# Which array shape TensorE's products take, and where attention's normalisation is written

## The chip, the core and the metric

One core of a Trainium2 chip. The metric is the device time of one execution in microseconds, the median over several runs; for a single run its one time. The engines are TensorE (PE, with PEld for its weight loads), VectorE (DVE), ScalarE (ACT), GpSimd (POOL) and the queue of SyncE (SP), which issues most DMAs. Each engine executes its instructions in the order of the program.

## The reference, cut to what matters

Attention inside clusters, and on its output a gated long convolution:

```python
# q, k, v: (4, 8, 768, 64); centroids: (8, 16, 64)
q_assign = argmax(q_n @ c_n.T); k_assign = argmax(k_n @ c_n.T)      # q_n, k_n, c_n: of unit length
mask = q_assign[:, :, :, None] == k_assign[:, :, None, :]
attn = softmax(where(mask, q @ k.T / 8, -1e9)); attn_out = attn @ v
x = attn_out.transpose(0, 2, 1, 3).reshape(4, 768, 512)
x1, x2, x3 = split(x @ w_proj, 3)
x2_conv = irfft(rfft(x2, axis=1) * rfft(filter_fft, axis=0), axis=1)
out = (x1 * x2_conv * x3) @ w_out
```

## The kernel before, in words

The 32 heads are taken in eight groups of four (n), each group in two pairs (pr), and in a pair the keys in six blocks of 128 (sk). The work is done in these steps.

Routing (`routing`, `first_masks`). Raw q and k are transposed on TensorE (`L570` in sixes, `L579` in threes), copied to SBUF (`qkT`) and cast to bf16 (`aug`). Products with the centroids (`sim`, L599) are copied out and transposed (`simT`, L610). VectorE makes one-hot rows of them (`oh`), TensorE transposes these (`ohT`), and DMAs set them into `aug` as extra rows, so that one product gives score and mask together.

Attention (`attention`). For each key block there are three score tiles of 512 columns (`sc`), three exponentials on ScalarE (`exp`, L695 and L698) into one of five buffers `p`, one group of value products in f32 (`pv`, L709, into a pair of PSUM banks, 4 and 5) and one addition into `acc` on VectorE (L719). After six blocks `acc` is summed over partitions (`den`, L732), and the pair is copied to `osb` (L724). The denominators are copied to SBUF. They go through DRAM to 12 columns, get eps added (L743), are inverted (L744), and come back through DRAM as rows over 64 partitions (`rb`). VectorE then adds eps to `osb` and multiplies it by `rb` in place (L780), and another instruction casts the result to bf16 as tokens (`xT`, line 789). The very last pair makes this turn on TensorE instead of through DRAM (L760, L765, L766, L772, L785).

Gated convolution (`hyena`), once for each batch b, behind its two head groups. `U` multiplies tokens by the middle third of w_proj (L817). `spectrum` is the forward transform (L464, L467). VectorE multiplies by the filter's spectrum (L841, L845). `G` gives the two gates, `I` the inverse transform, `fold` and L907 make `y2`, `W` is the output product. The first three batches' steps are spread among the attention of later groups. The last batch's steps come after all attention, so that the end of the program is a stage of its own, from the last `den` to the last output DMA.

The order of the work is drawn before anything is emitted. Every step is an `Op` with the engines it can run on and their costs, its inputs and outputs, its PSUM banks and a due time. `Plan.place` takes the steps one by one in simulated time: for the engine that can start first it takes the step with the earliest due time, with bonuses. On TensorE a step in another array shape than the last one is charged `switch`, and its due time is put off by `shape`. Six banks serve scores and all other products, at most four each; banks 4 and 5 are lent to early steps (class `head`) and are then the pair for `pv`.

TensorE's array is used in three shapes: whole (128 x 128) for transposes, in two halves (128 x 64) for `pv`, scores, projections and transforms, in four quarters (128 x 32) for `sim` and `den`. In halves, `columns` issues two matmuls for the two halves of the output rows, and they run beside each other:

```python
def columns(out, lhsT, rhs, start, stop):
    for i in range(2):
        tensor.matmul(out[64 * i:64 * i + 64], lhsT[:, 64 * i:64 * i + 64], rhs, start=start, stop=stop)
```

All helper calls of this kind are recorded under L63. A group of transposes takes up to three ready scores with it (`together`, `MIX`): their pieces of 256 columns are issued between the transposes with the whole array (L674, `woven`).

Of the kernel before, what the change touches and what calls it, by code (L numbers as in the profile page):

```python
# [35 lines left out]
MIX = 3  # L36
# [4 lines left out]
MODES = {"pv": (64, 64), "score": (64, 64), "bc": (64, 64), "inv": (64, 64), "proj": (64, 64), "sim": (32, 32),  # L41
         "den": (32, 32)}


class Op:
    __slots__ = ("eng", "fn", "due", "deps", "outs", "left", "ready", "end", "start", "on",
                 "alloc", "free", "lat", "lock", "byts", "seq", "kind", "parts", "group", "fused", "span")
# [10 lines left out]
def halves(tensor):  # L58


    def columns(out, lhsT, rhs, start, stop):
        for i in range(2):
            tensor.matmul(out[64 * i:64 * i + 64], lhsT[:, 64 * i:64 * i + 64], rhs, start=start, stop=stop)  # L63
    return columns


class Plan:
# [6 lines left out]
    def op(self, eng, fn, due, r=(), w=(), alloc=None, free=(), lock=False, byts=0, after=(), kind=None,  # L74
           parts=None):
# [4 lines left out]
        o.parts, o.group, o.fused = parts, [], False  # L80
# [22 lines left out]
    def place(self, free0, banks_for, switch=0.1, wait=0.1, rate=215e3, bonus=2.592, margin=0.43, shape=0.553):  # L103
# [26 lines left out]

        def together(o, t):

            for x in sorted((x for x in ready["PE"] if x.kind == "score" and x.ready <= t), key=lambda x: (x.due, x.seq)):
                ids = banks_for(x.alloc, bank_free, st, x)
                if ids is None or ids[1] > t or len(o.group) == MIX:
                    break
                take(x)
                x.fused = True
                o.group.append(x)
            a, b = len(o.parts), sum(len(x.parts) for x in o.group)  # L140
            return max(.056 * a + .109 * b, .108 * a + .055 * b) + (.05 if b else .14)
# [29 lines left out]
        while any(ready.values()):  # L171
            best = None
            for e, lst in ready.items():
# [14 lines left out]
                if not cand:  # L188
# [4 lines left out]
                    + (shape if e == "PE" and MODES.get(c[1].kind, (128, 128))[0] != st.last else 0.0)  # L193
# [8 lines left out]
            if e == "PE":  # L202
                mode, ends = MODES.get(o.kind, (128, 128))
                if o.parts and o.kind != "score":
                    d = together(o, t)
                o.span = d
                if mode != st.last:
                    d += switch
                st.last, st.kind = ends, o.kind
# [3 lines left out]
            for i, x in enumerate(o.group):  # L213
                done(x, e, t + 1e-6 * (i + 1), 0.0, t + d * (i + 1) / len(o.group))
# [3 lines left out]


def each(parts):  # L220
    def fn(e):
        for f in parts:
            f()
    return fn


def woven(a, b):

    out, i = [], 0
    for j, f in enumerate(b):  # L230
        out.append(f)
        while i * len(b) < (j + 1) * len(a):
            out.append(a[i])
            i += 1
    return out
# [27 lines left out]
def build(T):  # L263
# [3 lines left out]
    T0 = 10.36  # L267
    TAU1 = 3.298
    TAU2 = 3.626
# [11 lines left out]
    columns = lambda *a, **k: halves(T.nc.tensor)(*a, **k)  # L281
# [109 lines left out]
    def tables(got):  # L391
# [44 lines left out]
        for i in range(3):  # L436
            hs = [Bank("head"), Bank("head")]
            due = 34 + 4.0 * i
            for cs in range(2):
                op(("PE", .648), lambda e, i=i, cs=cs, h=hs[cs]: spectrum(ap(h), i, cs), due + 2 * cs, r=U2 + FW, w=[hs[cs]],  # L440
                   alloc=hs[cs], kind="proj")
# [111 lines left out]
    def routing(n):  # L553
# [5 lines left out]
        for u in range(8):  # L559
# [7 lines left out]
            if n > 1 and ch == 0:  # L567
                h = Bank(cls, 2)

                tr2 = [lambda i=i, s=s, h=h: T.nc.tensor.transpose(bank(h.ids[i // 3])[:, ts(i % 3, 128)], raw(s, i), T.ident)  # L570
                       for i in range(NT)]
                op(("PE", .80), each(tr2), due, r=[("qkraw", s, 0), ("qkraw", s, 1), "ident"], w=[h], alloc=h, parts=tr2)
# [3 lines left out]
            elif n < 2:  # L576
                h = Bank(cls)

                tr = [lambda t=t, s=s, ch=ch, h=h: T.nc.tensor.transpose(ap(h)[:, ts(t, 128)], raw(s, 3 * ch + t), T.ident)  # L579
                      for t in range(3)]  # L580
                op(("PE", .36), each(tr), due, r=[("qkraw", s, 0), ("qkraw", s, 1), "ident"], w=[h], alloc=h,
                   parts=tr if n else None)
                op(EV384 if n != 1 else {"ACT": .48}, lambda e, z=z, ch=ch, h=h: copy(e, T.qkT[z][:, ch], ap(h)[:, :384]),
                   due + .6, r=[h], w=[("qkT", z, ch)], free=[h])
# [8 lines left out]
        b0 = end - 23.512  # L593
# [9 lines left out]
        for ch in range(2):  # L603
# [6 lines left out]
        simT = [lambda i=i, h=h: T.nc.tensor.transpose(bank(h.ids[i // 3])[:, ts(i % 3, 128)],  # L610
                                                       T.sim[:, i // 3, ts(i % 3, 128)], T.ident) for i in range(NT)]
        op(("PE", .80), each(simT), b0 + 2.5, r=SIM + ["ident"], w=[h], alloc=h, parts=simT)
# [19 lines left out]
        def ohT(e, h=h):  # L632
            o = ap(h).bitcast(BF16)
            f = T.oh[:].rearrange("p a n c -> p (a n c)")
            for t in range(NT):
                for i in range(2):
                    c = 128 * t + 64 * i
                    T.nc.tensor.transpose(o[64 * i:64 * i + 64, ts(t, 128)], f[:, c:c + 64], T.identb)
# [16 lines left out]
    def attention(n, pr, sins):  # L655
# [7 lines left out]
        for sk in range(NT):  # L663
# [4 lines left out]
            for u in range(3):  # L668
                h = Bank("score")

                def piece(hp, c, lo, hi, sk=sk, h=h):
                    K = 80 if hp == 0 else 128
                    ag = T.augs[aset][pr][hp]
                    T.nc.tensor.matmul(ap(h)[:, c:c + hi - lo], ag[1][:K, ts(sk, 128)], ag[0][:K, lo:hi], start=True,  # L674
                                       stop=True)
                parts, c = [], 0
                for hp, lo, hi in THIRDS[u]:
                    parts += [lambda f=piece, a=(hp, c + x - lo, x, x + 256): f(*a) for x in range(lo, hi, 256)]
                    c += hi - lo

                def sc(e, u=u, sk=sk, h=h):
                    c = 0
                    for hp, lo, hi in THIRDS[u]:
# [5 lines left out]
                                                     for hp, _, _ in THIRDS[u]], w=[h], alloc=h, kind="score",  # L689
                   parts=parts)  # L690
# [44 lines left out]
        op(EV384, lambda e: copy(e, T.den, ap(h)[:, :384]), te + 1.5, r=[h], w=["den"], free=[h])  # L735
        if not last:
# [5 lines left out]
            def rec(e):  # L742
                T.nc.vector.tensor_scalar(T.dn, T.dn, EPS * S, None, op0=Alu.add)  # L743
                T.nc.vector.reciprocal(T.dn, T.dn)  # L744
            op(("DVE", .52), rec, te + 6, r=[], w=["dn"])
# [7 lines left out]
            rk, fr = [("rb", 0), ("rb", 1)], []  # L753
        else:
# [8 lines left out]
            def rec(e):  # L763
                V = T.nc.vector
                V.tensor_scalar(T.dn, ap(h2)[:, :384][:, ::32], EPS * S, None, op0=Alu.add)  # L765
                V.reciprocal(T.dn, T.dn)  # L766
            op(("DVE", .45), rec, te + 2.5, r=[h2], w=["dn"], free=[h2])
# [8 lines left out]
            fr = rk  # L776
        osv = lambda: T.osb[os][:, :, :384]
        eps = lambda: T.osb[os][:, 1, 384:385]
        if not last:
            op(("DVE", 1.05), lambda e: T.nc.vector.scalar_tensor_tensor(osv(), osv(), eps(), rbv(), op0=Alu.add,  # L780
                                                                         op1=Alu.mult),
               te + 12, r=rk, w=[("osb", os)], lock=True)
        else:
            for ch in range(2):
                op(("DVE", .6), lambda e, ch=ch: T.nc.vector.scalar_tensor_tensor(  # L785
                    osv()[:, ch], osv()[:, ch], eps(), ap(rk[ch])[:, :384], op0=Alu.add, op1=Alu.mult),
                   te + 4, r=[rk[ch]], w=[("osb", os)], free=[rk[ch]], lock=True)
        xs = b % 2
        op({"ACT": .83, "DVE": .55}, lambda e: copy(e, T.xT[xs][:, kt].rearrange("p (a b) -> p a b", a=2), osv()),
           te + 13 - 7 * last, r=[("osb", os)], w=[("xT", xs, kt)], lock=True)  # L790


    def hyena(b):
        xs = b % 2
        last = b == B - 1
        w0 = A(24 * (b + 1)) + 15.205
        w1 = A(24 * (b + 2)) + 7.046 if b < B - 2 else A(96) + 24.526
        if last:
            w0 = A(96) - 18.55
            w1 = w0 + 10  # L800
# [7 lines left out]
        for m in range(3):  # L808
            for w_ in range(2):
# [9 lines left out]
                if last and 2 * m + w_ < NU:  # L819
                    op(("PE", .647), lambda e, U=U: U(e, range(3)), due, r=XT[:3] + ["wpj"], w=[h], alloc=h, kind="proj")  # L820
                    op(("PE", .217), lambda e, U=U: U(e, range(3, 4)), due, r=[XT[3], h], w=[h], kind="proj")
                else:
                    op(("PE", .862), U, due, r=XT + ["wpj"], w=[h], alloc=h, kind="proj")
# [9 lines left out]
        for i in range(3):  # L833
            for cs in range(2):
# [4 lines left out]
                   w=[h], alloc=h, kind="proj")  # L839
# [223 lines left out]
def kernel(  # L1063
# [64 lines left out]
    for o in order:  # L1128
        if o.fused:
            continue  # L1130
        for x in [o] + o.group:
            if x.alloc is not None:
                psum.want(x.alloc)
        if o.group:
            each(woven(o.parts, sum((x.parts for x in o.group), [])))(o.on)
        else:
            o.fn(o.on)
# [30 lines left out]
```

The softmax here doesn't subtract the row's maximum and nothing guards it: scores larger than these inputs give would overflow.

## Time and profile before

| | |
|---|---|
| median of 8 runs | 402.72 us (401.63 to 404.54) |
| profiled execution | 402.58 us, its span 400.8 us |
| granted TensorE clock, mean over the span | 0.996 |
| busy TensorE / VectorE / ScalarE | 379.6 / 370.0 / 275.4 us |
| value products (L709) | 768 matmuls, 143.3 us busy |
| scores, projections, transforms (L63) | 69.1 + 51.9 + 23.7 us in the three largest groups |
| woven score pieces (L674) | 120 matmuls |
| casts of `osb` to `xT` | 15 on VectorE (560 ns each), 1 on ScalarE (832 ns) |
| eps added to 12 columns (L743, L765) | 16 on VectorE (165 and 161 ns) |

A line of a group names its line of code, engine, operation, tiles and shapes, the count, the busy time and the mean of one instruction, then the idle time before it and what ended it. A line of the timeline begins with start and length in microseconds. A shape such as 128*64 128x385 is that of the weights, then that of the moving data. The ends of matmuls are modelled, so their lengths overlap; the distances between starts are measured.

### The profile page before, as it was taken

How to read it: one execution, taken by the hardware profiler on the slowest of the kernel's cores; microseconds unless marked ns; L12 is line 12 of the kernel's file. 1: busy time of each engine (PE TensorE's matmuls, PEld its weight loads, DVE VectorE, ACT ScalarE, POOL GpSimd, SP SyncE). 2: the span in 40 equal slices, each digit the busy share in tenths (PEclk: the TensorE clock that was granted, in tenths of full speed). 3: DMA queues.
4: the chain of work that ended last, by engine and by line, in shares of the span. 5: the costliest groups of instructions: out<-in, count | busy, mean ns of one | idle time of the engine just before them, and what ended most of it. 6: DMA issues, size and time to landing. Idle time of an engine off the chain costs nothing.

```text
span 400.8 us, 8872 instructions
## 1 busy us (share of the span) xinstructions
PE 379.6 (95%) x3498; PEld 209.6 (52%) x3498; DVE 370.0 (92%) x513; ACT 275.4 (69%) x522; POOL 17.0 (4%) x55
## 2 busy tenths in 40 slices
PE   3989999999999999999999999999999999999963
PEld 2554553654455565654545565565555555645741
DVE  8899997988989999999899999998899999999992
ACT  4898778878855897677872778679855667523512
POOL 8700100000000000000000000000000000000000
PEclk9999999999999999999999999999999999999998
DMA  9939969118510433127522225104310101100304
GB/s 173 230 56 205 224 148 199 41 38 199 131 56 23 118 81 82 42 60 201 159 81 59 65 58 122 38 23 137 141 42 23 39 3 42 42 2 2 159 0 158
DMA packets 67233, 37.09 MB, mean 93 GB/s; under 512 B 56700, under 2 KB 62328, under 8 KB 67192
## 3 DMA queue, kind: packets, MB, share of 16 engines
q1 hardware_dynamic: 62856, 33.62, 32.2%
q0 software_dynamic: 1056, 2.10, 2.8%
q10 hardware_dynamic: 3280, 0.82, 1.1%
q8 instruction: 27, 0.44, 0.5%
q14 instruction: 14, 0.11, 0.1%
HBM read 30.66 MB, written 6.48 MB: 93 GB/s over the span
## 4 chain that ended last, share of the span: by engine, by line
PE 76%; DVE 13%; ACT 5%; issue 2%; DMA 1%; SPq 1%; POOL 0%; DVEq 0%; POOLq 0%; ACTq 0%
PE bank L63 28%; PE pair L709 27%; PE bank L817 5%; PE bank L674 3%; PE bank L570 3%; PE bank L599 3%; PE bank L732 2%; DVE acc L719 2%; ACT p L698 2%; PE bank L467 1%; PE bank L610 1%; DVE tm L841 1%; PE bank L493 1%; DMA rb<-dr 1%; DVE hm L454 1%
## 5 line engine op out<-in xcount | busy, mean ns | idle before, releaser
L709 PE MATMUL pair<-p,vraw 128*64 128x385 f32 x768 | 143.3, 489 | 0.0
L698 ACT ACTIVATE p<-bank 128x512 f32<-128x512 f32 x192 | 114.5, 619 | 29.6 <-PE bank L63 25.2
L719 DVE TENSOR_TENSOR acc<-p,acc 128x1536 f32<-128x1536 f32 x64 | 111.8, 1747 | 4.3 <-ACT p L698 2.9
L709 PEld LDWEIGHTS pair<-p,vraw 128*64 128x64 f32 x768 | 53.6, 136 | 44.9 <-issue 37.9
L63 PE MATMUL bank<-aug,aug 128*64 128x512 bf16 (+3 forms) x610 | 69.1, 327 | 1.4 <-DVE aug L536 0.7
L695 ACT ACTIVATE p<-bank 128x512 f32<-128x512 f32 x96 | 58.9, 613 | 4.2 <-PE bank L63 3.1
L63 PE MATMUL bank<-xT,wpj 128*64 128x384 bf16 x512 | 51.9, 327 | 0.1
L63 PEld LDWEIGHTS <-aug 128*64 128x64 bf16 (+1 forms) x610 | 35.3, 109 | 30.2 <-issue 17.5
L63 PEld LDWEIGHTS <-wpj 128*64 128x64 bf16 x512 | 28.0, 109 | 22.2 <-issue 13.4
L277 ACT COPY qkT<-bank 128x384 f32<-128x384 f32 x58 | 27.3, 498 | 10.5 <-PE bank L63 9.4
L63 PEld LDWEIGHTS <-y 128*64 128x64 bf16 x448 | 21.9, 110 | 17.2 <-issue 5.0
L719 DVE TENSOR_TENSOR acc<-p,p 128x1536 f32<-128x1536 f32 x16 | 28.0, 1752 | 1.8 <-ACT p L698 1.5
L674 PE MATMUL bank<-aug,aug 80*128 80x256 bf16 (+1 forms) x120 | 28.5, 274 | 0.1
L841 DVE TENSOR_TENSOR tm<-bank,hm 128x512 f32<-128x512 f32 x44 | 27.7, 681 | 0.0
L570 PE MATMUL bank<-ident,qkraw 128*128 128x128 f32 x144 | 27.1, 275 | 0.0
L63 PE MATMUL bank<-wout,y 128*64 128x512 bf16 x192 | 23.7, 381 | 3.3 <-DVE y L907 3.3
L277 ACT CAST aug<-qkT 64x768 bf16<-64x768 f32 x30 | 24.9, 831 | 2.6 <-DVE qkT L279 2.0
L817 PE MATMUL bank<-wpj,xT 128*64 128x512 bf16 x192 | 22.1, 380 | 1.0 <-DVE xT L279 1.0
L277 ACT COPY ob<-bank 128x512 f32<-128x512 f32 x20 | 11.5, 589 | 13.3 <-PE bank L63 13.2
L570 PEld LDWEIGHTS bank<-ident,qkraw 128*128 128x128 f32 x144 | 18.3, 141 | 3.8 <-issue 2.1
L279 DVE CAST aug<-qkT 64x768 bf16<-64x768 f32 x30 | 16.6, 552 | 2.4 <-ACT qkT L277 1.7
L724 ACT COPY osb<-pair 128x770 f32<-128x770 f32 x16 | 12.8, 800 | 8.6 <-PE pair L709 8.3
(145 smaller groups left out, 438.6 us busy)
## 6 DMA issues: line engine op xcount, KB each, us to landing
vraw<-in_v_dram SPq DMA_DIRECT2D x16, 384.0 KB
qkraw<-in_q_dram SPq DMA_DIRECT2D x30, 192.0 KB
qkraw<-in_k_dram SPq DMA_DIRECT2D x30, 192.0 KB
rb<-dr SPq DMA_DIRECT2D x30, 192.0 KB
out_dram<-ob SPq DMA_DIRECT2D x11, 512.0 KB
y<-in_moe_filter_fft_dram SPq DMA_DIRECT2D x4, 384.0 KB
wpj<-in_moe_w_proj_dram POOLq DMA_DIRECT2D x1, 1536.0 KB, 12.2
aug<-ohT SPq DMA_DIRECT2D x60, 24.0 KB
```

Of the source, the lines that this page charges most:

```text
L63: tensor.matmul(out[64 * i:64 * i + 64], lhsT[:, 64 * i:64 * i + 64], rhs, start=start, stop=stop)
L277: T.nc.scalar.copy(out, in_)
L279: (T.nc.vector if e == "DVE" else T.nc.gpsimd).tensor_copy(out, in_)
L570: tr2 = [lambda i=i, s=s, h=h: T.nc.tensor.transpose(bank(h.ids[i // 3])[:, ts(i % 3, 128)], raw(s, i), T.ident) for i in range(NT)]
L674: T.nc.tensor.matmul(ap(h)[:, c:c + hi - lo], ag[1][:K, ts(sk, 128)], ag[0][:K, lo:hi], start=True, stop=True)
L695: T.nc.scalar.activation(o, ap(h).rearrange("p (a b) -> p a b", a=2), Act.Exp, scale=0.125)
L698: T.nc.scalar.activation(flat(s)[:, lo:lo + 512], ap(h), Act.Exp, scale=0.125)
L709: T.nc.tensor.matmul(o[64 * hp:64 * hp + 64, ch, :385], T.vraw[vs][:, hp, sk * D:(sk + 1) * D], T.p[slots[sk]][:, hp, 384 * ch:384 * ch + ...
L719: T.nc.vector.tensor_tensor(T.acc[:], P_(t[0]), P_(t[1]) if len(t) == 2 else T.acc[:], op=Alu.add)
L724: op(("ACT", .83), lambda e: T.nc.scalar.copy(T.osb[os], two(ob)[:, :, :385]), te, r=[ob], w=[("osb", os)], free=[ob])
L817: T.nc.tensor.matmul(ap(h)[64 * i:64 * i + 64], T.xT[xs][:, kt, c:c + 64], T.wpj[:, kt, DM:2 * DM], start=kt == 0, stop=kt == ND - 1)
L841: op(("DVE", .68), lambda e, i=i, cs=cs, r=r, h=h: T.nc.vector.tensor_tensor(T.tm[r][:, cs], ap(h), hmrow(i, (0, 2, 2, 3)[2 * r + cs]), op ...
```

## The change

The weaving is taken out: `together`, `woven`, `each`, `MIX` and the 256-wide pieces go, and transposes are issued in plain groups. Scores, gates, output products, the first two spectra, the inverse transform and the transposes of the one-hot rows get no shape of their own: `array` gives them the shape that the step before left, where that is 128 or 64, and halves otherwise. `product` then issues one matmul on the whole array or two on halves. `U` and the third spectrum, whose two halves have different weights and moving data, stay in halves (kind `half`). The normalisation (L780, L785) writes `xT` in bf16 itself, and the cast goes. Eps is added where the denominators are copied out of PSUM, by an activation with a bias on ScalarE or an addition on VectorE, and L743 and L765 go. Some costs and due times of the planner are changed with it, so the order of the steps is drawn anew.

```diff
-MODES = {"pv": (64, 64), "score": (64, 64), "bc": (64, 64), "inv": (64, 64), "proj": (64, 64), "sim": (32, 32),
-         "den": (32, 32)}
+MODES = {"pv": 64, "bc": 64, "half": 64, "sim": 32, "den": 32, "score": 0, "proj": 0, "inv": 0}
+def array(o, last):
+    return MODES.get(o.kind, 128) or (last if last in (64, 128) else 64)
...
-def halves(tensor):
...
+def product(T, out, lhsT, rhs, start, stop):
+    if T.whole:
+        return T.nc.tensor.matmul(out, lhsT, rhs, start=start, stop=stop)
+    for i in range(2):
+        T.nc.tensor.matmul(out[64 * i:64 * i + 64], lhsT[:, 64 * i:64 * i + 64], rhs, start=start, stop=stop)
...
-    def place(self, free0, banks_for, switch=0.1, wait=0.1, rate=215e3, bonus=2.592, margin=0.43, shape=0.553):
+    def place(self, free0, banks_for, switch=0.1, wait=0.1, rate=215e3, bonus=2.592, margin=0.43, shape=0.33):
...
-                mode, ends = MODES.get(o.kind, (128, 128))
-                if o.parts and o.kind != "score":
-                    d = together(o, t)
-                o.span = d
+                mode = array(o, st.last)
                 if mode != st.last:
                     d += switch
-                st.last, st.kind = ends, o.kind
+                st.last, st.kind, o.whole = mode, o.kind, mode == 128
...
-    T0 = 10.36
-    TAU1 = 3.298
-    TAU2 = 3.626
+    T0 = 9.454
+    TAU1 = 3.31
+    TAU2 = 3.644
...
-                op(("PE", .80), each(tr2), due, r=[("qkraw", s, 0), ("qkraw", s, 1), "ident"], w=[h], alloc=h, parts=tr2)
+                op(("PE", .68), tr2, due, r=[("qkraw", s, 0), ("qkraw", s, 1), "ident"], w=[h], alloc=h)
...
-        b0 = end - 23.512
+        b0 = end - 24.593
...
-        op(EV384, lambda e: copy(e, T.den, ap(h)[:, :384]), te + 1.5, r=[h], w=["den"], free=[h])
+        def total(e):
+            if e == "ACT":
+                T.nc.scalar.activation(T.den, ap(h)[:, :384], Act.Copy, bias=EPS * S)
+            else:
+                T.nc.vector.tensor_scalar(T.den, ap(h)[:, :384], EPS * S, None, op0=Alu.add)
+        op(EV384, total, te + 1.5, r=[h], w=["den"], free=[h])
...
-            def rec(e):
-                T.nc.vector.tensor_scalar(T.dn, T.dn, EPS * S, None, op0=Alu.add)
-                T.nc.vector.reciprocal(T.dn, T.dn)
-            op(("DVE", .52), rec, te + 6, r=[], w=["dn"])
+            op(("DVE", .3), lambda e: T.nc.vector.reciprocal(T.dn, T.dn), te + 6, r=[], w=["dn"])
...
-        if not last:
-            op(("DVE", 1.05), lambda e: T.nc.vector.scalar_tensor_tensor(osv(), osv(), eps(), rbv(), op0=Alu.add,
-                                                                         op1=Alu.mult),
-               te + 12, r=rk, w=[("osb", os)], lock=True)
...
-        op({"ACT": .83, "DVE": .55}, lambda e: copy(e, T.xT[xs][:, kt].rearrange("p (a b) -> p a b", a=2), osv()),
-           te + 13 - 7 * last, r=[("osb", os)], w=[("xT", xs, kt)], lock=True)
+        xv = lambda: T.xT[xs][:, kt].rearrange("p (a b) -> p a b", a=2)
+        for a_ in [slice(0, 2)] if not last else [slice(0, 1), slice(1, 2)]:
+            op(("DVE", .6 if last else 1.05), lambda e, a_=a_: T.nc.vector.scalar_tensor_tensor(
+                xv()[:, a_], osv()[:, a_], eps(), ap(rk[a_.start])[:, :384].unsqueeze(1) if last else rbv(), op0=Alu.add,
+                op1=Alu.mult), te + (4 if last else 12), r=[("osb", os)] + (rk[a_] if last else rk), w=[("xT", xs, kt)],
+               free=rk[a_] if last else [], lock=True)
...
-        w0 = A(24 * (b + 1)) + 15.205
-        w1 = A(24 * (b + 2)) + 7.046 if b < B - 2 else A(96) + 24.526
+        w0 = A(24 * (b + 1)) + 18.221
+        w1 = A(24 * (b + 2)) + 14.861 if b < B - 2 else A(96) + 24.673
```

## The prediction

> **What bounds the kernel now.** I read the page first, its busy rows and its chain; then the groups by form; then the timeline at the places where the chain leaves TensorE.
>
> ```profile
> span 400.8 us, 8872 instructions
> PE 379.6 (95%) x3498; PEld 209.6 (52%) x3498; DVE 370.0 (92%) x513; ACT 275.4 (69%) x522; POOL 17.0 (4%) x55
> PEclk9999999999999999999999999999999999999998
> PE 76%; DVE 13%; ACT 5%; issue 2%; DMA 1%; SPq 1%; POOL 0%; DVEq 0%; POOLq 0%; ACTq 0%
> ```
>
> TensorE carries three quarters of the chain at the full granted clock; VectorE is nearly as busy but carries 13%. So one microsecond less on TensorE is one microsecond less where TensorE binds: from the first value product (31.2 us) to the last denominators (352.4). The head belongs to ScalarE, the end (347 to 389) half to VectorE. Two prices come from TensorE's timeline, read as start to next start, because ends are modelled:
>
> ```profile
> 151.28 1.46 PE L709 MATMUL pair<-p,vraw 128*64 128x385 f32 x8
> 152.58 0.82 PE L63 MATMUL bank<-xT,wpj 128*64 128x384 bf16 x8
> 155.20 1.46 PE L709 MATMUL pair<-p,vraw 128*64 128x385 f32 x8
> 156.58 1.50 PE L599 MATMUL bank<-qkT,cbd 128*32 128x384 f32 x16
> ...
> 150.30 0.27 PE L674 MATMUL bank<-aug,aug 128*128 128x256 bf16 x1
> 150.41 0.27 PE L570 MATMUL bank<-ident,qkraw 128*128 128x128 f32 x1
> 150.61 0.84 PE L63 MATMUL bank<-xT,wpj 128*64 128x384 bf16 x8
> ```
>
> The same eight value products take 1.30 us ahead of another 128x64 group and 1.38 ahead of a 128x32 one; after a woven transpose the next start is 0.11 us away in the same shape, 0.20 in another. Over all such pairs of the trace a change of shape costs 0.095 us. Woven pieces follow each other at 0.109 to 0.113 us, so weaving runs nothing beside anything: a 256-wide piece alone in two halves needs 0.107.
>
> Three waits matter besides: one bank release at 31, the routing at 64 to 67, the last tokens at 360.
>
> ```profile
> 30.48 0.65 ACT L277 COPY qkT<-bank 128x384 f32<-128x384 f32 x1
> 31.18 1.52 PE L709 MATMUL pair<-p,vraw 128*64 128x385 f32 x8
> 31.80 0.69 ACT L277 COPY qkT<-bank 128x384 f32<-128x384 f32 x1
> 64.45 1.48 PE L599 MATMUL bank<-qkT,cbd 128*32 128x384 f32 x10 [0.47 <-ACT qkT L277]
> 66.58 0.55 PE L610 MATMUL bank<-ident,sim 128*128 128x128 f32 x3 [0.17 <-DVE sim L279]
> 67.06 2.21 PE L63 MATMUL bank<-aug,aug 80*64 80x512 bf16 x18
> 354.35 0.56 DVE L279 CAST xT<-osb 128x768 bf16<-128x768 f32 x1
> 355.69 0.16 DVE L765 TENSOR_SCALAR dn<-bank 128x12 f32<-128x12 f32 x1
> 359.47 0.56 DVE L279 CAST xT<-osb 128x768 bf16<-128x768 f32 x1
> 360.08 2.13 PE L817 MATMUL bank<-wpj,xT 128*64 128x512 bf16 x18 [0.96 <-DVE xT L279]
> 361.41 0.68 DVE L830 TENSOR_TENSOR uv<-tm,bank 128x512 bf16<-128x512 f32 x1
> ```
>
> **The change part by part**, along the path first product (31.18) to last denominators (352.35) to end.
>
> *Array shapes.* In the issue order of the changed kernel TensorE changes shape 102 times instead of 123. Only the TensorE-bound stretch counts: 90 instead of 102. 12 x 0.095 = -1.1 us. In the head 8 instead of 17 changes lie beside ScalarE's exponentials: nothing, and at most -0.9 if that cover were gone.
>
> *No weaving.* In the stretch 58 of the 60 woven scores, 116 pieces, go from about 0.111 us to 0.107: -0.5 us.
>
> *Full-array products.* 89 product matmuls (44 scores and 8 projections or spectra) now use one 128x128 matmul where two 128x64 ones ran beside each other. No row shows a 512-wide one. Nearest are L674's full-array pieces: 0.109 us apart with weight loads of 0.097 in between, so the load is hidden even under a 256-wide piece. I take 0. The Trainium skill ("TensorE: Matmul & The Clock Gate", part 3, what overlaps and what doesn't) speaks against this: a weight load overlaps a running matmul only where the row group differs, and full-array matmuls share their row groups. By that rule some 65 of the 89 lie in the bound stretch and each shows its load: 65 x 0.097 = +6.3 us. The row is this kernel's own case, so it decides; the rule is a rival below. Below zero: two 512-wide half products also start 0.213 us after the pair before, the rate of one full product, so no gain is in sight.
>
> *Bank of the first value product.* The pair L709 writes needs banks 4 and 5, still lent to early transposes. Now the copy at 30.48 releases it, and L709 starts when it ends. In the new order the later transposed block, whose copy starts at 31.80, sits in bank 5, and ScalarE's order up to that copy is unchanged. The first product starts at about 31.80 + 0.65 = 32.4: +1.2 us. Queued behind it are the 96 value products and the score buffers they free. Ends: 0 (ScalarE gets there sooner) and +1.4.
>
> *Routing at 57 to 68.* By starts, TensorE stands 2.25 us here: 0.2 for the denominators, 1.2 around L599, 0.3 between the halves of L610, 0.5 for exponentials after ScalarE had waited 1.71 for scores. In the new order scores follow L599 directly and L610 comes 22 operations later, behind four value products. L610's waits go, and ScalarE starts earlier; the wait for L599's input stays: -0.9 us (ends -0.3 and -1.5).
>
> *Work moved across the borders.* One score (0.21) goes ahead of the first product, one L63 group of the last batch's gates (0.64) goes behind the last denominators: -0.85 for the stretch. Together: -1.1 - 0.5 + 1.2 - 0.9 - 0.85 = -2.15; last denominators at 350.2.
>
> *VectorE and the queues.* Off go 15 casts to xT (0.56), one on ScalarE (0.83), 16 eps additions (0.16): 11 us of VectorE. The normalisation now writes bf16: by rows L830 and L841, same size to bf16 and to f32, 681 ns each, that is free (ends 0 and 15 x 0.1, hidden all the same). Adding eps at the denominators' copy makes a ScalarE copy of 0.48 an activation; the exponentials, 0.61 against 0.585 for a copy of that size, say +0.03, at most +0.1, in front of DMAs. All that lies beside TensorE, except in the last stage. On SP the eight mask copies for the second head group pass one load of v whose first use is over 30 us later: nothing. POOL's queue is unchanged.
>
> *The last stage.* From last denominators to first U part with the last tokens took 7.7 us (352.35 to 360.08), VectorE's chain throughout. The two casts and the addition, 1.3 us, are gone, and one fold of 0.5 no longer sits between the two last normalisations. TensorE's own work becomes the limit: denominators 0.65, two gate groups 1.28, transposes 0.33, three U groups 1.92, broadcasts 1.28, four shape changes 0.38 = 5.8 us. So U comes 1.9 earlier. But the new order leaves two VectorE instructions of the batch before for after the U stage: L907 (0.87 by its pitch) and one L881 (0.47). They had filled VectorE's wait for U; now they stand in front of the chain that ends in the last y. -1.9 + 1.35 = -0.55. One od copy moves from ScalarE to VectorE (0 to +0.5; a wait of 0.43 for the twin copy on ScalarE follows, so 0). The tail gives -0.55 (ends -1.3 and +0.5).
>
> Sum: -2.15 - 0.55 = **-2.7 us**. The profiled execution took 402.58 us, span 400.8 and 1.8 around it, 0.14 below the median of 402.72. 402.58 - 2.7 = 399.9.
>
> **The rivals.**
>
> *Late again elsewhere* (2 in 10). Every engine issues in order, and the order was drawn anew everywhere. At 224 us TensorE lost 0.26 to one late VectorE instruction. Ten such places, or one exponential chain late by 2 us, would leave 400.9 to 402.8. For: VectorE 92% busy. Against: it gets 11 us of air, and TensorE hardly waits from 70 to 345.
>
> *Weight loads shown* (7 in 100). The rule above holds for full products: +6.3 - 2.7 = +3.6, 406.2. It decides from 28 exposed loads in the bound stretch on (28 x 0.097 = 2.7). Against: L674's spacing.
>
> *More than summed* (15 in 100). The bank comes free as early as now (-1.2), the routing wait goes whole (-1.35): 397.4. For: both steps were priced with care on the dear side. Against: the position of the copy in ScalarE's order is plain.
>
> *It does nothing to the shapes*: excluded by the counts of the issue order.
>
> **How the numbers follow.** The main case has 58 in 100: 398.3 to 401.5 by the ends of its steps. A difference of 0.3%, 1.2 us, is about what a measurement of this kernel tells from no change. Faster: 56 of the main case, 15 of the third rival, 5 of the first: 76. Same: 2 and 13: 15. Slower: 7 and 2: 9. The range leaves out about 1 in 10 on each side: 397.0 to 403.0.
>
> **What would show it.** In the changed profile: about 100 shape changes, full-array score matmuls spaced 0.213 us at 512 wide (0.31 would be the rule); the first L709 at 32 to 32.5; scores directly behind the routing product near 64; the last denominators near 350; no cast to xT, U within 6 us of the denominators; VectorE 359 us busy. Wrong it is if the first product is on time, if TensorE waits between 70 and 345 for more than 2 us, or if the stretch from U to the last y grows by more than 1.4.

## The result and the profile after

| | before | after |
|---|---|---|
| median | 402.85 us (401.11 to 404.83, 32 runs) | 399.92 us (398.41 to 402.16, 11 runs) |
| ratio, 95% interval | | 0.9936 [0.9921, 0.9952] |
| profiled execution, its span | 402.58, 400.8 us | 399.49, 397.7 us |
| first value product | 31.18 us | 31.60 us |
| last denominators | 352.35 us | 347.95 us |
| first `uv` of the last batch (U with the last tokens done) | 361.41 us | 355.01 us |
| last wait for `y` ends | 389.03 us | 384.26 us |
| last matmul | 393.59 us | 390.50 us |

The median is 2.9 us lower, and in the pair of profiles the difference is 3.1 us. The forecast was 399.9. The stages did not go as forecast, though: the last denominators came 2.25 us earlier than said, and behind them 1.85 us of that was lost again. From the page of the changed kernel, its busy row, clock row and the shares of the chain:

```profile
span 397.7 us, 8781 instructions
PE 378.1 (95%) x3447; PEld 205.0 (52%) x3447; DVE 360.8 (91%) x485; ACT 274.4 (69%) x518; POOL 17.1 (4%) x55
PEclk9999999999999999999999999999999999999988
PE 90%; DVE 5%; ACT 3%; issue 1%; POOL 0%; POOLq 0%; DVEq 0%; ACTq 0%
```

VectorE lost 9 us of work, TensorE 1.5; the chain runs 90% through TensorE where it ran 76%. New is the 8 in the last but one slice of the clock: the granted clock fell inside the work. The places that had waits before, in the timeline (start, length, then in brackets the idle time before it and what ended it):

```profile
31.09 0.45 ACT L244 COPY qkT<-bank 128x384 f32<-128x384 f32 x1
31.60 1.52 PE L668 MATMUL pair<-p,vraw 128*64 128x385 f32 x8 [0.95 <-ACT qkT L244]
...
63.00 1.79 PE L567 MATMUL bank<-qkT,cbd 128*32 128x384 f32 x16
64.72 2.48 PE L68 MATMUL bank<-aug,aug 80*64 80x512 bf16 x24
```

The first value product (L668, in the kernel before L709) waits for the copy that the prediction named. At the routing (L567, in the kernel before L599) no bracket is left: scores follow directly, and the wait for L567's input, which the prediction let stand, is gone too. The view of waits has no line at all for TensorE from 33 to 345 us. The last stage, TensorE and VectorE, and as the last row the output products of the kernel before:

```profile
347.95 0.85 PE L691 MATMUL bank<-acc,ones 128*32 128x384 f32 x8
351.31 1.48 PE L731 MATMUL bank<-ident,dn 128*64 128x128 f32 x24
352.25 1.27 DVE L740 SCALAR_TENSOR_TENSOR xT<-osb,bank 128x384 bf16<-128x384 f32 x2
355.01 1.29 DVE L783 TENSOR_TENSOR uv<-tm,bank 128x512 bf16<-128x512 f32 x2 [1.49 <-ACT tm L244]
...
384.26 6.62 PE L68 MATMUL bank<-wout,y 128*64 128x512 bf16 x44 [3.26 <-DVE y L860]
```

```profile
389.03 4.94 PE L63 MATMUL bank<-wout,y 128*64 128x512 bf16 x44 [3.26 <-DVE y L907]
```

No cast stands between L740 and the products; from denominators to `uv` it takes 7.06 us instead of 9.06. The surprise is the output products: 44 matmuls in 6.62 us, where before they took 4.94 behind a wait of the same length.

### The profile page after: what moved, and what is told of

The parts are those of the page before. It is cut to its first block, busy times and chain, and to the rows that moved or that the text cites. A ratio compares the mean times of both kernels' runs of the same rounds, so it can differ in the third digit from the quotient of the medians.

```text
span 397.7 us, 8781 instructions
## 1 busy us (share of the span) xinstructions
PE 378.1 (95%) x3447; PEld 205.0 (52%) x3447; DVE 360.8 (91%) x485; ACT 274.4 (69%) x518; POOL 17.1 (4%) x55
## 4 chain that ended last, share of the span: by engine, by line
PE 90%; DVE 5%; ACT 3%; issue 1%; POOL 0%; POOLq 0%; DVEq 0%; ACTq 0%
PE bank L68 34%; PE pair L668 32%; PE bank L770 5%; PE bank L539 5%; PE bank L691 3%; PE bank L66 3%; PE bank L567 3%; PE bank L434 2%; ACT p L657 1%; PE bank L580 1%; ACT p L654 1%; PE bank L608 1%; ACT qkT L244 1%; DVE ob L338 1%; DVE ob L331 0%
## 5 line engine op out<-in xcount | busy, mean ns | idle before, releaser
L668 PE MATMUL pair<-p,vraw 128*64 128x385 f32 x768 | 141.8, 490 | 0.9 <-ACT qkT L244 0.9
L668 PEld LDWEIGHTS pair<-p,vraw 128*64 128x64 f32 x768 | 52.1, 136 | 48.5 <-issue 40.9
L68 PE MATMUL bank<-aug,aug 128*64 128x256 bf16 (+3 forms) x654 | 69.9, 326 | 0.1
L68 PE MATMUL bank<-xT,wpj 128*64 128x384 bf16 x480 | 48.0, 326 | 0.0
L244 ACT COPY qkT<-bank 128x384 f32<-128x384 f32 x55 | 25.1, 486 | 16.3 <-PE bank L539 6.2
L244 ACT CAST aug<-qkT 64x768 bf16<-64x768 f32 x36 | 30.0, 833 | 2.3 <-DVE qkT L246 1.7
L68 PE MATMUL bank<-wout,y 128*64 128x512 bf16 x160 | 21.2, 405 | 3.5 <-DVE y L860 3.5
L539 PE MATMUL bank<-ident,qkraw 128*128 128x128 f32 x144 | 20.0, 280 | 0.0
L539 PEld LDWEIGHTS bank<-ident,qkraw 128*128 128x128 f32 x144 | 15.5, 140 | 8.5 <-issue 3.0
L783 DVE TENSOR_TENSOR uv<-tm,bank 128x512 bf16<-128x512 f32 x24 | 15.3, 683 | 4.0 <-PE bank L770 2.1
L770 PEld LDWEIGHTS <-xT 128*64 128x64 bf16 x192 | 10.7, 110 | 10.8 <-issue 3.1
```

Source lines behind the costliest of these rows:

```text
L68: T.nc.tensor.matmul(out[64 * i:64 * i + 64], lhsT[:, 64 * i:64 * i + 64], rhs, start=start, stop=stop)
L244: T.nc.scalar.copy(out, in_)
L668: T.nc.tensor.matmul(o[64 * hp:64 * hp + 64, ch, :385], T.vraw[vs][:, hp, sk * D:(sk + 1) * D], T.p[slots[sk]][:, hp, 384 * ch:384 * ch + ...
L770: T.nc.tensor.matmul(ap(h)[64 * i:64 * i + 64], T.xT[xs][:, kt, c:c + 64], T.wpj[:, kt, DM:2 * DM], start=kt == 0, stop=kt == ND - 1)
L783: op(("DVE", .68), lambda e, m=m, e_=e_, o_=o_, h=h: T.nc.vector.tensor_tensor(T.uv2[:, e_, m], T.tm[m % 2][:, 0], ap(h), op=o_), due + 1, ...
```

## The experiments

The theory to test is that of the prediction: TensorE binds the long middle, so fewer shape changes and waits count there in full, and VectorE's relief only in the last stage. Its rivals: exposed weight loads, and a VectorE that decides in the middle as well.

The marks of the table above (first value product, last denominators, `uv`) cut each profile into the stretch bound by TensorE, the last stage, and the rest. The stretch is then counted from starts. Its streaming time is what its columns take at the pace of full groups (0.213 us for 512). A start that comes later than the streaming ahead of it allows is late. A late start where the shape changes is put down to the change, up to some 0.1 us; beyond that, or elsewhere by over 60 ns, it is a wait. The rest is late starts under 60 ns.

| the stretch | before | after |
|---|---|---|
| streaming | 299.5 us | 298.7 us |
| late starts at changes of shape | 10.5 us, 103 changes | 9.3 us, 90 changes |
| waits over 60 ns | 3.6 us | 0.8 us |
| the rest, under 60 ns each | 7.5 us | 7.5 us |

### Four single runs that take the change apart

**The normalisation alone**, in the order of the kernel before:

```diff
-    scalar_tensor_tensor(osv(), osv(), eps(), rbv(), ...); copy(e, T.xT[...], osv())
+    scalar_tensor_tensor(xv(), osv(), eps(), rbv(), ...)
-    copy(e, T.den, ap(h)[:, :384]);  ... tensor_scalar(T.dn, T.dn, EPS * S, ...)
+    activation(T.den, ap(h)[:, :384], Act.Copy, bias=EPS * S)      # or a VectorE addition
```

> The kernel before in its own issue order, with only the normalisation's edits: xT written in bf16 directly, no cast, eps at the denominators' copy. Theory (VectorE binds only in the last stage): first value product and last denominators stay within 0.3 us of 31.2 and 352.4; the stretch from last denominators to the first uv on VectorE falls from 9.1 to about 7.9 us, because TensorE's own 6.5 us there becomes the limit; no leftover y stands in front, so about -1.1 us in all. Rival (the cast is hidden anyway): nothing moves, 0. Rival (VectorE's 11 us count on the way too): last denominators 2 us or more earlier.

Measured: 401.55 us; the stretch 320.6 us (321.2 before), denominators to `uv` 7.86 us instead of 9.06. As the theory had it, in this order. The normalisation costs nothing more for writing bf16: 1012 ns in this run and 1011 in the changed kernel, where the f32 form took 1013. The row of the changed kernel:

```profile
L740 DVE SCALAR_TENSOR_TENSOR xT<-osb,rb 128x768 bf16<-128x768 f32 x15 | 15.2, 1011 | 0.0
```

**Plain groups and whole-array products alone**, in the order of the kernel before:

```diff
-    each(woven(o.parts, sum((x.parts for x in o.group), [])))(o.on)
+    each(o.parts)(o.on)                       # the transposes, then
+    for x in o.group: x.fn(o.on)              # their scores, whole-array at 512 columns
```

> The kernel before in its own issue order, but each group issues its transposes plainly and then its scores as whole-array products of up to 512 columns instead of woven 256-wide pieces. Theory: shape changes unchanged, 58 scores in the bound stretch cost 0.213 us instead of 2 x 0.111, so from first value product to last denominators about -0.5 us, total -0.5. Rival (a whole-array product shows its weight load): about 77 matmuls x 0.097 = +7 us. Rival (weaving hid something): +0.3 us for every group of six transposes and three scores, +4 us.

Measured: 406.45 us; the stretch 322.7 us, 1.5 longer. None of the three expected sizes came. The loads are not shown (they would have cost 7 us). The view of waits for TensorE from 33 to 345 us has lines that the kernel before lacks:

```profile
PE bank L63 <- DVE tm L845: 0.7, 1, 0.7
PE bank L63 <- ACT p L699: 0.3, 1, 0.3
PE bank L736 <- DVE acc L723: 0.2, 1, 0.2
```

So the prediction's -0.5 for the weaving is not found. A reading that fits is that woven scores come out before the end of the transposes, and that VectorE's chains stood on that; no run separates it, and part of the 1.5 us may be the execution's: the stretch of the kernel before, unchanged, shows a wait of 0.4 us on VectorE in a later profile (that with idle products, below) which its first one lacks. (From the last denominators to the last matmul it took 2.75 us more: two windows of half clock at the end, of which below.)

**The cast back, in the changed order**: straight behind each normalisation, on VectorE, and the additions of eps before the reciprocals. The order was left as it was drawn without them.

```diff
-    scalar_tensor_tensor(xv()[:, a_], osv()[:, a_], eps(), ...)
+    scalar_tensor_tensor(osv()[:, a_], osv()[:, a_], eps(), ...); copy(e, xv(), osv())
```

> The changed kernel in its own issue order, with the cast to xT (always on VectorE, straight behind the normalisation) and the eps additions on the 12 columns put back. Theory: first value product and last denominators within 0.4 us of 31.6 and 348.0; the stretch from last denominators to the first uv grows from 7.1 us by 0.6 to 1.3, and the end with it, since VectorE's chain behind it is full: total +0.6 to +1.3 us at the same granted clock. Rival (hidden): 0. Rival (VectorE counts everywhere): +5 us or more before the last denominators.

Measured: 407.48 us; the stretch 322.4 us instead of 316.4. The theory fell and the rival was right. The four longest of TensorE's waits from 70 to 345 us, where the view of the changed kernel has none:

```profile
PE bank L691 <- DVE acc L678: 1.2, 3, 0.5
PE bank L68 <- DVE sd L858: 1.0, 2, 0.6
PE bank L608 <- DVE oh L597: 0.7, 2, 0.5
PE pair L668 <- ACT osb L683: 0.6, 1, 0.6
```

Its streaming is that of the changed kernel, so the 6 us are late starts, and most of those listed end with VectorE. VectorE's 11 us lay beside TensorE in the old order; the new order has spent them.

**40 scores more on the whole array**, between groups in halves, to price a change of shape:

```diff
+    if pe[i].kind == "score" and all(narrow(pe[j]) for j in (i - 1, i, i + 1)): pe[i].whole = True   # 40 times
```

> The changed kernel in its own issue order, but 40 scores that stand between products in halves are issued on the whole array, so that TensorE changes shape 80 times more in the bound stretch. Theory (0.095 us per change, whole-array products as fast as two halves): first value product to last denominators +7.6 us, from 316.4 to 324.0. Rival (changes are hidden by the queue): below +2. Rival (whole-array products show a weight load): 7.6 + 52 x 0.097 = +12.6 us.

Measured: 409.49 us; the stretch 325.3 us, +8.9 for 80 changes, nearest to the main expectation (+7.6). The late starts at changes grew by 8.35 us, 0.104 each.

```profile
179.68 0.49 PE L68 MATMUL bank<-xT,wpj 128*64 128x384 bf16 x4
180.10 0.39 PE L66 MATMUL bank<-aug,aug 80*128 80x512 bf16 x1
180.42 0.63 PE L68 MATMUL bank<-aug,aug 80*64 80x256 bf16 x6
```

The one whole score holds TensorE for 0.32 us: 0.215 of its own and 0.1 for the way back.

### The end of the program: the clock

> The changed kernel once more, as the yardstick for the runs beside it: about 0.993 to 0.994 of the time before (400 us). Theory of the clock at the end: TensorE stands some 3.4 us for the last tokens before the first product with the output weights, and the records then show half clock for one window of 3.4 us (or two), within which the pairs of output products start 0.427 us apart instead of 0.213.

This is the changed kernel once more. Measured: 400.35 us (399.41 to 401.73, 6 runs), ratio 0.9931 [0.9904, 0.9958]; again there is one window of half clock, 385.3 to 388.7 us. The busy time in windows of the changed kernel (first profile; the number behind POOL is the granted clock):

```profile
core 0: us, PE busy (x) PEld busy (x) DVE busy (x) ACT busy (x) POOL busy (x), PEclk, DMA share, GB/s
381.10:384.50 3.40, 0.24 (x3) 0.14 (x5) 3.40 (x7) 0.00 (x0) 0.00 (x0) 1.00 0.00 0
384.60:388.00 3.40, 3.40 (x20) 1.46 (x18) 2.06 (x4) 0.00 (x0) 0.00 (x0) 0.50 0.00 0
```

A window of 3.4 us with 0.24 us of work at full clock, and then one full of work at half of it. To take the idle window away, 14 idle matmuls go before the first output product of the last batch:

```diff
+    if last and tt == 0 and e_ == 0 and 0 in kts:
+        for _ in range(14): tensor.matmul(ap(h), T.wpj[:, 0, :128], T.wpj[:, 0, :512], start=True, stop=True)
```

> The changed kernel with 14 idle 512-wide full-array products (0.215 us each, about 3.0 us) in the bank of the first output product of the last batch, put directly before it, so that TensorE works while it waits for the last tokens. Theory (the wait halves the clock): no half clock between 384 and 391 us, output pairs at 0.213, the stretch from the wait's end to the last matmul 4.9 us instead of 6.6; about 398.3 us, 1.6 less than the changed kernel (ratio about 0.989), and less spread. Rival (the clock falls for another reason, or the slower tail is only of the profiled execution): the time of the changed kernel within 0.4 us.

Measured: 398.16 us (397.99 to 399.69, 4 runs), ratio 0.9883 [0.9852, 0.9914]: as the theory had it. One of the four took 399.69 at a mean clock of 0.991, so a window can still be lost. In the timeline of the profiled run (all lines one higher in the file):

```profile
380.44 3.19 PE L874 MATMUL bank<-wpj 128*128 128x512 bf16 x13
383.56 0.62 PE L69 MATMUL bank<-wout,y 128*64 128x512 bf16 x4
384.59 4.94 PE L69 MATMUL bank<-wout,y 128*64 128x512 bf16 x44 [0.41 <-DVE y L861]
```

The same 44 matmuls now take 4.94 us again.

> The kernel before with the same 14 idle products before its first output product of the last batch. Its profiled execution showed no half clock there, but its times spread over 3 us. Theory of the clock: its median falls by less than the changed kernel's does, between 0 and 1.7 us, and its spread shrinks. Rival (the clock has no part in it): the time of before, or 0 to 0.4 us more for the idle products.

Measured: 401.47 us (400.95 to 401.93, 13 runs), ratio 0.9959 [0.9945, 0.9974]. 1.7 us less, at the edge of what was expected, and a spread of 1 us instead of 3. So the kernel before often loses such a window too, and its first profile was spared. Its other times say the same: of 20 runs of it, the four with a mean clock of 0.996 took 401.36 to 402.00 us, the sixteen with 0.989 to 0.993 took 402.61 to 403.83. With the clock held up in both, the change is worth 401.47 - 398.16 = 3.3 us.

### The bank of the first value product

```diff
+    tr.alloc.ids, sc.alloc.ids = sc.alloc.ids, tr.alloc.ids     # last early transposed block 5 -> 6, a score 6 -> 5
```

> The changed kernel, with the banks of the last early transposed block and of the second score of that block exchanged, so that the first value product no longer needs the bank of the later copy. Theory of the prediction (the first product waits for that copy, and everything behind it is bound by TensorE): first value product at 30.7 instead of 31.6 us, and the last denominators and the end earlier by the same 0.9 us: 399.0 us. Rival (the waits behind it take the gain up: the routing's input and ScalarE's exponentials are late by as much): first product at 30.7, but the last denominators within 0.3 us of the changed kernel's.

Measured: 399.37 us (398.79 to 401.59, 6 runs), ratio 0.9913 [0.9884, 0.9941], against 400.35 for the changed kernel on the same chip. The first product is at 31.32 us, because the first score came late in this execution (21.70); from first score to first value product it takes 9.62 us instead of 10.45: the bank costs 0.83, near the 0.9 of the theory. In the profiled execution the gain was lost at 91 us, where the masks of the next pair came late:

```profile
90.96 0.84 PE L68 MATMUL bank<-aug,aug 80*64 80x512 bf16 x6 [0.92 <-DMA aug<-ohT]
```

That left open whether it is lost always, so it was run with the clock held up:

> The changed kernel with the 14 idle products before the first output product and with the two early banks exchanged, to be read against the run with the idle products alone (398.16 us). Theory of the prediction (all behind the first value product is bound by TensorE): the first product is 0.83 us nearer to the first score, and the end comes earlier by as much: 397.3 us. Rival (given back: in the profile of the exchange without idle products the mask DMAs at 91 us came 1.1 us late and took all of it): the time within 0.3 us of 398.2, with a DMA wait near 91 in the profile again.

Measured: 397.70 us (397.33 to 398.30, 5 runs), ratio 0.9877 [0.9853, 0.9902]; the lowest time of all versions, though its interval covers that of the idle products alone. The long DMA wait did not come again (0.17 us at 89.7). From first score to last matmul 367.42 us against 367.88: of 0.83 us, 0.46 arrive. Between the two expectations, then: about half is given back to later waits, by 90 us already.

### Whole array or halves, in the same order

```diff
-    T.whole = o.on == "PE" and o.whole
+    T.whole = o.on == "PE" and o.whole and o.kind is None      # products always in halves
```

> The changed kernel with the idle products before the first output product, its issue order kept to the instruction, but every product that went as one 128x128 matmul now as two 128x64 ones. Theory of the prediction (a whole-array product costs the same as two half ones; only shape changes count): about 3 more changes behind the first value product, +0.3 us there, the time within 0.6 us of 398.16. Rival of the exposed weight loads: the halves are faster, by up to 6 us less in that stretch. Rival that the whole-array form itself brings the gain: the stretch longer by 1.5 us or more.

Measured: 399.20 us (398.15 to 400.20, 6 runs), ratio 0.9910 [0.9886, 0.9934]. The same ten products, first with whole-array products (the changed kernel with idle products), then in halves:

```profile
187.76 0.38 PE L67 MATMUL bank<-aug,aug 128*128 128x512 bf16 x1
187.98 1.03 PE L67 MATMUL bank<-wout,y 128*128 128x512 bf16 x3
188.84 0.38 PE L67 MATMUL bank<-aug,aug 80*128 80x512 bf16 x1
189.06 1.03 PE L67 MATMUL bank<-wout,y 128*128 128x512 bf16 x4
```

```profile
189.97 0.41 PE L69 MATMUL bank<-aug,aug 128*64 128x512 bf16 x2
190.21 1.03 PE L69 MATMUL bank<-wout,y 128*64 128x512 bf16 x8
191.07 0.39 PE L69 MATMUL bank<-aug,aug 80*64 80x512 bf16 x2
191.29 1.03 PE L69 MATMUL bank<-wout,y 128*64 128x512 bf16 x8
```

From the first score to the second, 1.08 us whole and 1.10 in halves; four output products take 0.86 us either way, although each whole one has a weight load of 97 ns before it. (The x3 lacks one record.) So a whole product costs what two halves cost, and its load is hidden. The median is higher by 1.0 us all the same, because the profiled execution had a window of half clock at the first value product (32.1 to 35.5 us), and the two others of 399.8 and 399.9 us have a mean clock as low (0.991). The three runs with a mean clock of 0.996 or more took 398.15 to 398.61, against 397.99 to 398.17 for the three best with whole products: +0.3 us, about the price of the four changes more in the stretch (94 for 90).

### Order and shapes without the normalisation

The changed kernel with cast and eps additions as steps of their own again, known to the planner, which draws the order anew:

```diff
-    op(("DVE", 1.05), ... scalar_tensor_tensor(xv()...), w=[("xT", xs, kt)])
+    op(("DVE", 1.05), ... scalar_tensor_tensor(osv()...), w=[("osb", os)])
+    op({"ACT": .83, "DVE": .55}, lambda e: copy(e, xv(), osv()), ..., w=[("xT", xs, kt)])
```

> The changed kernel with the idle products before the first output product, but the normalisation undone in the order's making too: the value is normalised in f32, cast by an operation of its own (VectorE or ScalarE), eps added before the reciprocal; the order is drawn anew with these. Plain groups and shapes as changed (105 changes in all against 102). Theory that the order and the shapes alone bring the gain of the bound stretch: from first value product to last denominators about 317 us (316.4 in the changed kernel, 321.2 before), waits above 60 ns under 1.5 us, and only the last stage gives up its 1.3 to 2 us: about 400 us. Rival that the stretch needs VectorE's freed 11 us: waits ended by VectorE of 3 us or more between 70 and 345, the stretch at 320 or more: 403 us or more.

Measured: 404.62 us (402.77 to 406.24, 15 runs), ratio 1.0038 [1.0020, 1.0055]: slower than the kernel before, and slower than that kernel with idle products (401.47) even in the six runs with a clock of 0.996 or more, 402.77 to 403.87. The first theory fell. The rival named the time, not quite the place: TensorE has 94 changes in the stretch and loses little to waits until 345 us, and then stands where VectorE is behind.

```profile
351.64 2.12 PE L69 MATMUL bank<-xT,wpj 128*64 128x384 bf16 x24
355.04 0.85 PE L692 MATMUL bank<-acc,ones 128*32 128x384 f32 x8 [1.29 <-DVE acc L679]
356.48 0.55 PE L723 MATMUL bank<-ident,den 128*128 128x128 f32 x3 [0.59 <-ACT den L245]
```

```profile
351.28 3.62 DVE L679 TENSOR_TENSOR acc<-p,acc 128x1536 f32<-128x1536 f32 x2
354.81 0.55 DVE L840 TENSOR_TENSOR x<-bank,x 128x384 f32<-128x384 f32 x1
```

VectorE has no wait here from 344 to 358 us. The last denominators start at 355.04, 7.1 us later than in the changed kernel. Besides the 1.3 us of this wait these are 1.2 us more of waits ahead of it, 1.9 us of streaming that this order puts into the stretch, 0.4 for four more changes, 0.4 at the first value product, and a window of half clock there (31.6 to 35.0 us). `uv` follows 8.8 us behind the denominators.

The fourth corner of the square is the normalisation alone with the clock held up:

> The kernel before, its order untouched, with the normalisation edits alone (bf16 written directly, no cast, eps at the evacuation) and the 14 idle products before the first output product. It is the fourth corner of a square: neither part 401.47 us, both parts 398.16, order and shapes alone 404.62 (403.2 in its undisturbed runs). Theory that the two parts need each other (the redrawn order spends what the normalisation frees, and earns nothing without): the normalisation alone gives what its last stage and the small waits give, about 2.2 us by the profile without idle products: 399.3 us, so the parts' single effects (-2.2 and +1.7 or more) sum to far less than the -3.3 of both. Rival that the effects add: -3.3 - 1.7 = -5.0 for the normalisation alone, 396.5 us.

Measured: 400.04 us (399.78 to 400.22, 6 runs), ratio 0.9932 [0.9912, 0.9952]. That is -1.4 us against 401.47 instead of the -2.2 expected, and far from the -5.0 of effects that add.

| with idle products | order of before | order drawn anew, new shapes |
|---|---|---|
| cast and eps as before | 401.47 us | 404.62 us (402.77 to 403.87 at full clock) |
| normalisation writes bf16 | 400.04 us | 398.16 us |

The normalisation is worth 1.4 us in the old order, and in the new one 6.5 by the medians or 4.9 by the six runs at full clock (median 403.03). The new order and shapes cost 3.2 or 1.6 us without it, and bring 1.9 with it. One limit of this: the order without the normalisation was drawn with the due times of the changed kernel. Whether other due times would draw a better one for a VectorE with more to do was not tried, so the 4.9 to 6.5 us are the worth in this planning.

## Why the prediction was right, and where only its sum was

*Shape changes* (-1.1). Right: 13 fewer in the stretch, and their late starts fell from 10.5 to 9.3 us, -1.2; the run with 80 more gives 0.104 us each. (In the head the traces show 14 instead of 18, where the prediction had 8 instead of 17; it had put no time on these.)

*No weaving* (-0.5). Not found. The step took the spacing of woven pieces for the whole effect. With plain groups in the old order the stretch grew by 1.5 us instead, in one run; why is not shown. Late starts under 60 ns stayed at 7.5 us.

*Whole-array products* (0). Right: 1.08 against 1.10 us in the pair above. The rule weighed there, from the Trainium skill ("TensorE: Matmul & The Clock Gate", Part 3), that a weight load overlaps a running matmul only where the row group differs, would have made a whole product 0.31 us by these rows (0.215 and a load of 0.097); 0.215 was measured, with the load under it.

*Bank of the first product* (+1.2, first product at 32.4). The mechanism holds, and the exchange of banks priced it at 0.83. The product came at 31.60 for another reason: the profile of before, from which the step was read, was itself late here. Its first transposes started 0.48 us later than in that of the changed kernel, and ran at half clock until 15.3 us (the other profiles here: until 10.7 to 13.9); it took 11.30 us from the first transpose to the first of the routing, where all others but one (9.91) took 10.6 to 10.7. Counted from that routing transpose, the first product is 1.6 us later after the change; from the span's start, 0.4. Before, then after:

```profile
16.77 0.59 PE L503 MATMUL bank<-ident,sim 64*128 64x64 f32 x6
20.89 0.79 ACT L277 COPY aug<-bank 16x768 bf16<-16x768 bf16 x1
23.34 0.60 ACT L698 ACTIVATE p<-bank 128x512 f32<-128x512 f32 x1
```

```profile
15.63 0.58 PE L470 MATMUL bank<-ident,sim 64*128 64x64 f32 x6
20.65 0.79 ACT L244 COPY aug<-bank 16x768 bf16<-16x768 bf16 x1 [0.94 <-DVE aug L246]
22.82 0.58 ACT L657 ACTIVATE p<-bank 128x512 f32<-128x512 f32 x1
```

What the step left out is ScalarE's start. In the new order its copy of mask rows waits 0.94 us for VectorE's. So the first exponential comes 7.19 us behind the routing transpose instead of 6.57, although the first score comes 0.6 us sooner (5.5 instead of 6.1). From the first exponential to the first product it takes 8.78 us instead of 7.84, of which the bank is 0.83. So the +1.2 was 0.4 too small for an equal start; that the product came 0.8 sooner than said is luck of the profile.

*Routing* (-0.9, ends -0.3 and -1.5). Mis-sized, and outside its ends: by starts, waits at 57 to 71 us fell from 2.5 to 0.5 us. The wait for L599's input was said to stay and went.

*Work moved* (-0.85). Right: the streaming time of the stretch is 0.85 us less.

*VectorE's 11 us lie beside TensorE.* This was the step that failed as a statement on the change. It was read from the profile of before, and holds in its order (-0.6 us in the stretch). The order after is another one, drawn for a VectorE with less to do; with the cast put back into it the stretch is 6 us longer. The third rival, "more than summed", comes nearest in the stretch, at -4.8 us where the sum had -3.35 (-1.1, -0.5, -0.9 and -0.85). The rival that lateness returns elsewhere did not come in the stretch: the view of waits has none of TensorE from 70 to 345 us. The runs with the cast say why: without VectorE's freed time this order waits.

*The last stage* (-0.55). `uv` is 2.0 us nearer to the denominators (1.9 said), and the wait for the last `y` ends 36.31 us after them instead of 36.68: -0.4. So this step held. What was missing stands behind it: the output products at half clock, +1.7 us, a term that the prediction does not have. The profile of before has 3.26 us of wait at this place, with full clock behind it. The Trainium skill ("TensorE: Matmul & The Clock Gate", Part 1) says that a window of about 3.4 us without work halves the clock. The changed kernel's window had 0.24 us of work in it, so here a wait that does not quite fill one was enough. The spread of 3 us in the times of before was the sign.

So: 350.2 forecast for the last denominators, 347.95 measured; -0.55 forecast behind them, +1.3 measured. The forecast of -2.7 met -3.1 in the profiles because two errors of about 2 us had opposite signs: that the total is so near is luck.

## What to carry to other kernels

Time freed on an engine off the path buys little in an order drawn without it (1.4 us here), and can carry the gain of an order drawn with it: cost the parts of such a change together, and ask in which order the cover that you read will exist. Before a short burst on TensorE, look how long it stood: a wait of 3 us costs its own length and can then cost half the clock for the next window (up to 1.7 us here), and idle matmuls into the bank that the burst is about to write cost nothing that shows here. A matmul on the whole array took here what two halves side by side take; what costs is the change of shape, 0.1 us each time.

## What the runs showed of the hardware

The granted clock changes in windows of 3.41 us that lie at another place in each execution: half clock from 384.6 to 388.0, from 385.3 to 388.7, and in one profile of the bank exchange for two windows, 384.2 to 391.0. It is not a matter of a full idle window only. Both kernels below have the idle products. With products in halves, a window at the first value product with TensorE busy for 1.90 of 3.40 us by its records was followed by half clock; with whole products one with 1.98 was not:

```profile
28.70:32.10 3.40, 1.90 (x14) 0.69 (x13) 3.29 (x3) 3.37 (x9) 0.00 (x0) 1.00 0.60 139
32.10:35.50 3.40, 3.40 (x16) 0.98 (x20) 2.82 (x4) 2.23 (x4) 0.00 (x0) 0.50 1.03 267
```

```profile
29.30:32.70 3.40, 1.98 (x10) 0.68 (x10) 3.28 (x4) 3.36 (x8) 0.00 (x0) 1.00 0.78 212
32.70:36.10 3.40, 3.40 (x29) 0.97 (x26) 3.34 (x4) 2.62 (x5) 0.00 (x0) 1.00 1.03 227
```

Where the threshold lies stays open: another window, with 2.21 us busy (28.2 to 31.6 us in the order drawn anew with the cast), was followed by half clock, and one of before with 1.77 (387.4 to 390.8 us) by full clock. The records overlap, so they are no exact measure of it. What the runs show is the size: up to 1.7 us for each window at half clock, which is half its length.
